# Two decode layers with sliding-window attention: V as the moving operand in seven heads of the first attention, one matmul each for the mask and the q block

## The chip, the cores and the metric

The kernel runs on one core of a Trainium2 chip. The metric is the device time of one execution in microseconds; the time given for a kernel is the median of its runs. The five engines are named as in the profile: PE (TensorE, with PEld for its weight loads), DVE (VectorE), ACT (ScalarE), POOL (GpSimd) and SP (SyncE, which here only issues DMAs).

## What is computed

Four sequences take one decode step through attention, GLU, attention, GLU, with the same weights and the same cache both times:

```python
W = min(4096, max(256, Sk // 4))            # 2048 of 8192 cached positions
q = (x @ wq).reshape(B, Sq, Hq, Dh)         # B 4, Sq 1, Hq 32, Dh 128
k = repeat(k_cache[:, :, Sk - W:, :], 4)    # 8 kv heads, 4 q heads on each
v = repeat(v_cache[:, :, Sk - W:, :], 4)
p = softmax((q @ k.T) * Dh ** -0.5)
attention = (p @ v).reshape(B, Sq, Hq * Dh) @ wo
glu = (sigmoid(g) * u) @ w_down             # g = x @ w_gate, u = x @ w_up, width 1792

x = x + attention(layernorm(x)); x = x + glu(layernorm(x))
x = x + attention(layernorm(x)); x = x + glu(layernorm(x))
```

Everything is bf16 in memory; D is 512. The K window and the V window are 16 MB each, wq and wo 4 MB each, the GLU weights 5.5 MB together.

## The kernel before, in words

**Memory.** One arena of 50 slots of 4 KB per partition (512 KB each) holds what is loaded. Slots 0 to 31 keep the whole K window, loaded once and used by both attentions. The other 18 slots are 9 pairs of 1 MB, given out by a small pool: a load takes a free pair, and the pair goes back when its last reader is done (`done`, `give`, `fill`, lines 450 to 473). The four Wo pairs stay until the second attention has used them. Towards the end of the first attention some loads are given fixed half pairs as homes (`load_half`, line 487): halves of Y (V of head 7, first pair), Z (head 7, second), GA (head 6, first) and GB, a pair that the loads list takes from the pool behind the last Wo load (line 1439). All big loads are issued by SP in the order of one list (lines 1428 to 1453): wq, K two heads ahead of V, Wo every second head, V; then the GLU weights, wq again, the second V pass from head 7 down, the GLU weights again. V of head 7 and parts of head 6 stay on the chip between the two attentions, some of them parked in PSUM by DVE transposes (`stash`, `stash_half`).

**Planning.** Every operation is entered in a plan with an engine, an estimated duration, what it reads and writes, and the PSUM banks that it touches. `_schedule` then makes one fixed order for each engine from estimated times, and `_assign_sync` puts in the waits. On the chip each engine runs its list in order. So an estimate changes the order of instructions, not what they do; SP keeps the list's order whatever the estimates are.

**One head of the first attention** (`attn_first`, line 1171). `k_transpose`: four DVE transposes turn the K of the head (line 854). `q_unit` (834): four matmuls write the q of the head into the four diagonal blocks of a block matrix in PSUM, the zeros with it, and one ACT copy of 128x256 brings it to `qbd`. `softmax_unit` (861): four matmuls of 32 rows add the mask (872), sixteen the scores (883), then DVE takes the maximum in five small steps (896 to 908), and ACT the exponential with the row sums (911). `turn_p` (922): a permutation matmul, an ACT copy and a DVE transpose give the probabilities in the layout that PV needs. `pv_unit` (960): **V is the stationary operand**; 32 matmuls for each of the two V pairs of the head load 128x128 of V as weights and move 8 columns of probabilities (973). Then DVE scales by the reciprocal of the sums (`oe`, 981), four matmuls permute (991), DVE masks (`oq`, 996), and `wo_unit` multiplies by Wo in sixteen matmuls with Wo as weights (1162), collecting in one PSUM bank. The loop prepares the scores of head h+2 before PV of head h.

**One head of the second attention** (`attn_second`, line 1201) for the first seven of its heads is in the wide form. `pv_wide` (1041): **V is the moving operand**; sixteen matmuls take 32 columns of probabilities as weights and move 512 columns of V, four side by side on different columns of the PE array (1055). DVE transposes the 128x512 result (`tv`, 1064), reduces it to its diagonal (`rd`, 1069) and shifts half of it (`sh`, 1071); POOL adds and scales (`ad`, `av`, 1073 and 1076); two matmuls and an ACT copy bring it into the layout for Wo (`tr`, `oc`, 1090 and 1096); `wo_wide` needs four matmuls with Wo moving (1109), collected in another bank that `wo_copy` and `wo_back` fold in at the end (1136, 1146). The last two of the seven use `wo_compact` (1125), sixteen matmuls with Wo as weights. `sums` (1023) does the row sums on POOL with one small f32 matmul, where `sums_old` (936) splits them in three bf16 parts. The wide form's intermediate results live in `wide_buffers`, laid over an arena slot.

## Time and profile before

| | |
|---|---|
| median of the runs | 178.71 us (178.64, 178.71, 178.74) |
| the profiled execution | 178.76 us, of which the span from first to last instruction is 177.0 |
| read from HBM | 70.26 MB |
| DVE in first attention, 20 to 40 and 60 to 80 us | 15.21 and 12.85 of 20 us busy |
| PE in the same stages | 11.35 and 7.60 of 20 us busy |
| DVE in second attention, 130 to 150 us | 18.70 of 20 us busy |
| first attention ends (its last Wo matmuls) | 105.03 us |
| second attention ends (its last Wo matmuls) | 164.73 us |
| last matmul of the kernel | ends about 174.65 us |

How to read it: times in the views are microseconds from the first instruction, so they add up to the span and not to the execution's time. The page cuts the span into 40 slices of 4.43 us and gives each engine's busy share in tenths. A row of a group view gives the line in the kernel, the engine, the operation with its output and inputs, the number of instructions, their busy time, the mean duration of one in ns, the time that the engine stood idle just before them and what it waited for.

### The profile page before, as it was taken

What the parts mean: (1) busy time and instruction counts of PE and PEld (TensorE: products, weight loads), DVE (VectorE), ACT (ScalarE), POOL (GpSimd) and SP (SyncE); (2) the same over time, 40 slices, a digit from 0 to 9 for tenths busy, and PEclk for the clock granted to TensorE, in tenths of its full rate; (3) what the DMA queues carried; (4) which work ended last, traced back from release to release, by engine and by line L of the source; (5) the groups of instructions that cost most, each with busy time, mean ns of one, the idle gap of its engine ahead of it and who ended that gap; (6) DMA issues with size and microseconds to landing.
All of it is one profiled execution on the core that took longest, in us unless ns stands there. A gap on an engine that the chain in (4) does not pass through costs nothing.

```text
span 177.0 us, 3893 instructions
## 1 busy us (share of the span) xinstructions
PE 102.3 (58%) x1641; PEld 55.0 (31%) x1653; DVE 104.6 (59%) x256; ACT 32.7 (18%) x87; POOL 21.6 (12%) x88
## 2 busy tenths in 40 slices
PE   0536236382842634607418866456886999776663
PEld 0203112241431431603404852052323444435322
DVE  7307997838477375594383772304299999742351
ACT  2002031312030210300301101000043365430011
POOL 6100010101010100100100100000011454342000
PEclk9999999999999999999999999999999999975555
DMA  6999999999999999999999999999999999999980
GB/s 179 418 429 428 420 422 416 416 420 426 411 414 429 415 422 418 415 420 426 411 420 428 400 403 403 409 401 387 404 429 409 420 418 422 413 417 405 413 351 28
DMA packets 12882, 70.52 MB, mean 398 GB/s; under 512 B 1336, under 2 KB 1344, under 8 KB 6720
## 3 DMA queue, kind: packets, MB, share of 16 engines
q1 hardware_dynamic: 12856, 70.26, 97.4%
q8 instruction: 13, 0.21, 0.5%
q14 instruction: 5, 0.04, 0.1%
q10 hardware_dynamic: 8, 0.00, 0.0%
HBM read 70.26 MB, written 0.00 MB: 397 GB/s over the span
## 4 chain that ended last, share of the span: by engine, by line
DMA 38%; DVE 32%; PE 18%; issue 4%; SPq 4%; ACT 2%; DVEq 0%; ACTq 0%
DMA arena<-in_B_w_down_dram 15%; DMA arena<-in_A_v_cache_dram 15%; DVE arena L854 11%; PE ps L883 7%; DVE nmax L896 5%; DMA arena<-in_B_w_gate_dram 4%; DMA arena<-in_A_wq_dram 4%; SPq L398 4%; PE ps L973 3%; PE ps L872 2%; DVE nmax L900 2%; DVE mxt L904 2%; DVE ebuf L931 2%; PE ps L1162 2%; DVE arena L1064 2%
## 5 line engine op out<-in xcount | busy, mean ns | idle before, releaser
L854 DVE STREAM_TRANSPOSE arena<-arena 128x1024 f32<-128x1024 f32 x32 | 37.0, 1202 | 0.0
L883 PE MATMUL ps<-arena,qbd 128*32 128x512 bf16 x256 | 25.6, 537 | 0.0
L896 DVE TENSOR_REDUCE nmax<-ps 128x1 f32<-128x512 f32 x16 | 10.8, 675 | 19.4 <-PE ps L883 19.3
L973 PE MATMUL ps<-ebuf,arena 128*128 128x8 bf16 x576 | 17.7, 168 | 7.5 <-DMA arena<-in_A_v_cache_dram 4.4
L872 PE MATMUL ps<-msk_m,msk_s 128*32 128x512 bf16 x64 | 8.6, 526 | 23.1 <-DVE arena L854 21.8
L973 PEld LDWEIGHTS ps<-ebuf,arena 128*128 128x128 bf16 x576 | 16.8, 104 | 9.5 <-DMA arena<-in_A_v_cache_dram 5.5
L911 ACT ACTIVATE prow<-ps,nmax 128x512 bf16<-128x512 f32 x16 | 11.0, 687 | 35.1 <-DVE nmax L908 29.5
L847 ACT CAST qbd<-ps 128x256 bf16<-128x256 f32 x16 | 5.9, 370 | 45.0 <-PE ps L883 35.1
L940 POOL CAST s<-psm 128x1 bf16<-128x1 f32 x9 | 1.7, 187 | 84.0 <-ACT prow L911 84.0
L883 PEld LDWEIGHTS ps<-arena,qbd 128*32 128x32 bf16 x256 | 8.4, 121 | 10.4 <-issue 7.7
L795 PE MATMUL ps<-arena,xn 128*4 128x512 bf16 x64 | 8.5, 572 | 4.9 <-DMA arena<-in_A_wq_dram 4.4
L926 ACT CAST prow<-ps 128x512 bf16<-128x512 f32 x16 | 9.4, 585 | 9.9 <-PE ps L973 2.1
L1342 PE MATMUL ps<-arena,xn 128*4 128x448 bf16 x64 | 7.7, 547 | 4.2 <-DMA arena<-in_B_w_up_dram 1.9
L931 DVE STREAM_TRANSPOSE ebuf<-prow 128x256 f32<-128x256 f32 x16 | 7.0, 435 | 3.8 <-ACT prow L926 3.7
L872 PEld LDWEIGHTS ps<-msk_m,msk_s 128*32 128x32 bf16 x64 | 1.7, 98 | 24.1 <-DVE arena L854 22.7
L773 ACT ACTIVATE lnv<-ps 128x4 f32<-128x4 f32 x4 | 0.7, 173 | 41.0 <-PE ps L769 41.0
L1055 PE MATMUL ps<-arena,ebuf 128*32 128x512 bf16 x112 | 7.9, 405 | 0.2 <-DVE nmax L908 0.2
L842 PE MATMUL ps<-qh,eyew 32*128 32x64 bf16 x64 | 5.6, 217 | 3.7 <-ACT qbd L847 2.4
L807 DVE STREAM_TRANSPOSE ebuf<-ps 128x512 f32<-128x512 f32 x3 | 2.1, 717 | 9.4 <-PE ps L795 9.3
L1351 DVE STREAM_TRANSPOSE ebuf<-ps 128x448 f32<-128x448 f32 x4 | 2.6, 650 | 7.1 <-PE ps L1342 7.1
L1162 PE MATMUL ps<-onp,arena 128*128 128x16 bf16 x144 | 5.3, 175 | 2.5 <-DVE onp L996 2.2
L981 DVE TENSOR_TENSOR onb<-ps,rinv 128x16 bf16<-128x16 f32 x9 | 1.7, 185 | 8.3 <-PE ps L973 8.1
(112 smaller groups left out, 132.2 us busy)
## 6 DMA issues: line engine op xcount, KB each, us to landing
arena<-in_A_v_cache_dram SPq DMA_DIRECT2D x27, 1024.0 KB, 22.4
arena<-in_A_k_cache_dram SPq DMA_DIRECT2D x16, 1024.0 KB, 25.1
arena<-in_A_wq_dram SPq DMA_DIRECT2D x4, 1024.0 KB, 8.0
arena<-in_A_wq_dram SPq DMA_DIRECT2D x8, 512.0 KB, 6.2
arena<-in_A_wo_dram SPq DMA_DIRECT2D x3, 1024.0 KB, 26.2
arena<-in_B_w_down_dram SPq DMA_DIRECT2D x4, 512.0 KB, 6.4
arena<-in_B_w_gate_dram SPq DMA_DIRECT2D x4, 448.0 KB, 8.3
arena<-in_B_w_up_dram SPq DMA_DIRECT2D x4, 448.0 KB, 6.2
```

The costliest lines, as they stand in the source:

```text
L795: last = pe.matmul(ps[32 * hh:32 * hh + NB, qb, :], xn[:, c * NB:(c + 1) * NB], src[:, o + hh * 512:o + (hh + 1) * 512], start=(c == 0), s ...
L854: P.op("vector", "T%d_%d" % (h, t), c_dve(1024), lambda v, v32=v32: v.transpose(v32, v32), r=[("slot", 4 * h + t)], w=[("slot", 4 * h + t)])
L872: last = pe.matmul(ps[32 * gi:32 * gi + 32, bank, :], msk_s[:, :], msk_m[:, :].unsqueeze(1).broadcast_to([128, 256, 2]), start=True, stop= ...
L883: last = pe.matmul(ps[32 * gi:32 * gi + 32, bank, :], qbd[:, q0:q0 + 32], kt[:, cp // 2, cp % 2, jh * NJ:(jh + 1) * NJ, :], start=False, s ...
L896: lambda v: v.tensor_reduce(nmax[:, k2:k2 + 1], ps[:, bank, :], AXX, ALU.max),
L911: lambda a: a.activation(prow[:, :].rearrange("p (m x t) -> p m x t", x=32, t=2), ps[:, bank, :].rearrange("p (m t x) -> p m x t", x=32, t ...
L926: P.op("scalar", "pc" + tag, c_act(512), lambda a: a.copy(prow[:, :], ps[:, pb, :]), r=[("ppb", pb)], w=[("prow",)], banks=(pb,))
L931: P.op("vector", "pt" + tag, c_dve(256), lambda v: v.transpose(et, prow[:, :].bitcast(F32)), r=[("prow",)], w=[("e", k2)])
L973: last = pe.matmul(ps[:, ob, bp * 8:bp * 8 + 8], src[:, j * 128:(j + 1) * 128], ev[:, j % 2, j % 16 // 2, x0:x0 + 8], start=(j == 0), stop ...
L1055: last = pe.matmul(ps[32 * g:32 * g + 32, ob, :], ew[:, g, mq, t], src.rearrange("p (m t d) -> p t m d", t=2, d=128)[:, t], start=(n == 0) ...
L1162: last = pe.matmul(ps[:, WB, c * NR:(c + 1) * NR], tile_ap(s)[:, o + r_ * D + c * 128:o + r_ * D + (c + 1) * 128], ov[:, r_ * NR:(r_ + 1) ...
L1342: last = pe.matmul(ps[32 * g:32 * g + NB, gub[n], 0:NF], xn[:, c * NB:(c + 1) * NB], slot_ap(s)[:, g * NF:(g + 1) * NF], start=(c == 0), s ...
```

## The change

The first attention's heads 0 to 6 use the wide form (`pv_wide`, `sums`, `o_back`, then `wo_wide` for heads 0 to 4 and `wo_compact` for 5 and 6); head 7 keeps the old form. All of them share one wide buffer, a half of pair GB, so GB is taken from the pool before anything is loaded, and its other half is free for a weight half from the start. Homes of the half loads are dealt out anew. The PV of head 5 is issued in two parts, one for each V pair; the other wide heads read both pairs in one operation. All four parts of V of head 7 are parked before its results are scaled.

The mask becomes one matmul with 128 weight columns in place of four with 32. The q of a head becomes one matmul of 64 columns, and four ACT copies put its 32-row blocks on the diagonal of `qbd`, whose zeros are set once at the start and again after the first GLU, which overlays it. Both hold in both attentions; the copies are issued one head ahead in the first. The zeroing of PSUM at the start covers four banks instead of three. Estimates for the first attention are given separately from those for the second (`est`), which bears on the order alone; the wide buffer index is 0 there (`kb`).

```diff
-        msk_s = sb("msk_s", [128, 32], BF16)
+        msk_s = sb("msk_s", [128, 128], BF16)
...
+        def est(tag, first, rest_):
+            return first if tag[0] == "0" else rest_
+
+        def kb(tag, k2):
+            return 0 if tag[0] == "0" else k2
...
-                                  (((Y, 1), (GB, 0), (GB, 1), (GA, 0)), ((GB, 0), (GB, 1), (GA, 0), (Y, 0)))[i][c])
+                                  (((GB, 0), (GB, 1), (GA, 0), (Y, 0)), ((GB, 1), (GA, 0), (Y, 0), (Y, 1)))[i][c])
...
-                                  (((GB, 0), (GB, 1), (GA, 0), (Y, 0)), ((Y, 1), (Z, 0), (GB, 0), (GB, 1)))[nm == "wu"][c])
+                                  (((GB, 1), (GA, 0), (Y, 0), (Y, 1)), ((GB, 0), (Z, 0), (GB, 1), (GA, 0)))[nm == "wu"][c])
...
-        P.op("vector", "zero_o", 1100.0, lambda v: v.memset(ps[:, OBS[0]:WB + 1, :], 0.0), w=[("o0",)], banks=OBS + (WB,))
+        P.op("vector", "zero_o", 1450.0, lambda v: v.memset(ps[:, PBS[1]:WB + 1, :], 0.0), w=[("o0",)], banks=(PBS[1],) + OBS + (WB,))
...
+        P.op("vector", "eye4", 100.0,
+             lambda v: v.tensor_copy(eyew[:, 32:128].rearrange("p (a j) -> p a j", a=3),
+                                     eyew[:, 0:32].unsqueeze(1).broadcast_to([128, 3, 32])),
+             r=[("eyew",)], w=[("eye4",)])
...
-            def e_qx(pe):
-                last = None
-                for a in range(4):
-                    last = pe.matmul(dst[:, :, a * REP:(a + 1) * REP], eyew[32 * hh:32 * hh + 32, 96 - 32 * a:224 - 32 * a],
-                                     src, start=True, stop=True)
-                return last
-            P.op("tensor", "qx" + tag, 250.0, e_qx, r=[("qh", h // 4), ("eyew",)], w=[("cb",)], banks=(CB,))
-            P.op("scalar", "qe" + tag, c_act(256),
-                 lambda a: a.copy(qbd[:, k2 * 256:(k2 + 1) * 256], ps[:, CB, 0:256]),
-                 r=[("cb",)], w=[("q", k2)], banks=(CB,))
+            P.op("tensor", "qx" + tag, 200.0,
+                 lambda pe: pe.matmul(ps[:, CB, 0:64], eyew[32 * hh:32 * hh + 32, :], src, start=True, stop=True),
+                 r=[("qh", h // 4), ("eyew",), ("eye4",)], w=[("cb",)], banks=(CB,))
+            dst = qbd[:, k2 * 256:(k2 + 1) * 256].rearrange("p (x y) -> p x y", y=NR)
+            for a in range(4):
+                P.op("scalar", "qe%d%s" % (a, tag), 200.0,
+                     lambda e, a=a: e.copy(dst[32 * a:32 * a + 32, :, a * REP:(a + 1) * REP],
+                                           ps[32 * a:32 * a + 32, CB, 0:64].rearrange("p (x r) -> p x r", r=REP)),
+                     r=[("cb",)], w=[("q", k2, a)], banks=(CB,))
...
             def e_m(pe):
-                last = None
-                for gi in range(4):
-                    last = pe.matmul(ps[32 * gi:32 * gi + 32, bank, :], msk_s[:, :],
-                                     msk_m[:, :].unsqueeze(1).broadcast_to([128, 256, 2]), start=True, stop=False)
-                return last
+                return pe.matmul(ps[:, bank, :], msk_s[:, :], msk_m[:, :].unsqueeze(1).broadcast_to([128, 256, 2]),
+                                 start=True, stop=False, skip_group_check=True)
...
+            for bps in ((0,), (1,)) if tag == "0.%d" % (NF1 - 2) else ((0, 1),):
+                P.op("tensor", "PV" + tag, est(tag, 1950.0, 16 * tm["pe_row"]), lambda pe, bps=bps: e_pv(pe, bps),
...
+        NF1 = HKV - 1
+
         def attn_first():
+            slot = base[GB]
+            begin = len(P.ops)
+            wide_buffers([slot], P.ops[-1])
+
             def front(h):
                 k_transpose(h)
-                softmax_unit("0.%d" % h, h)
-                turn = lambda: turn_p(0, "0.%d" % h, h % 2, PBS[h % 2])
-                return turn
-
+                softmax_unit("0.%d" % h, h, q=False)
+                if h + 1 < HKV:
+                    q_unit("0.%d" % (h + 1), h + 1, (h + 1) % 2)
+                return lambda: turn_p(0, "0.%d" % h, h % 2, PBS[0], h < NF1)
...
+                pv_wide(tag, h, h % 2, v_tiles[(0, h)])
                 if turn is not None:
                     turn()
-                wo_unit(tag, h, op, h % 2, False, h == HKV - 1)
+                op = late.pop(("tr", tag))()
+                if h < NF1 - 2:
+                    wo_wide(tag, h, op, h % 2, h == 0, h == NF1 - 3)
+                    if h == NF1 - 3:
+                        wo_copy(0)
+                        wo_back(0, False)
+                else:
+                    wo_compact(tag, h, op, h % 2)
+            wide_done()
+            h, tag = NF1, "0.%d" % NF1
+            st = [stash(stashed, (n,)) for n in range(4)]
+            need(Z)
+            op = pv_unit(tag, h, h % 2, v_tiles[(0, h)])
+            oe, oq = named("oe" + tag), named("oq" + tag)
+            oe[0].deps.update(st)
...
+            if not last:
+                P.op("gpsimd", "qbd1", 200.0, lambda g: g.memset(qbd[:, 0:2 * NH], 0.0),
+                     w=[("q", 0, a) for a in range(4)])
...
-        loads.append((GB, lambda s: None))
...
+        base[GB] = pool.alloc()
+        hfree.add(base[GB] + 1)
         fill()
```

## The prediction

> **What bounds the kernel now.** I read the page first: busy shares, the 40 slices, the DMA queues.
>
> ```profile
> span 177.0 us, 3893 instructions
> PE 102.3 (58%) x1641; PEld 55.0 (31%) x1653; DVE 104.6 (59%) x256; ACT 32.7 (18%) x87; POOL 21.6 (12%) x88
> DMA  6999999999999999999999999999999999999980
> GB/s 179 418 429 428 420 422 416 416 420 426 411 414 429 415 422 418 415 420 426 411 420 428 400 403 403 409 401 387 404 429 409 420 418 422 413 417 405 413 351 28
> q1 hardware_dynamic: 12856, 70.26, 97.4%
> q8 instruction: 13, 0.21, 0.5%
> ```
>
> No engine is busy over 59%, while the 16 DMA engines are full in 37 of 40 slices: loads take 97.4% of their span. 70.26 MB at the 415 GB/s of the full slices is 169 us; what is left is the start (first issue at 0.79 us, slice 0 at 179 GB/s) and the tail. So a stage can be shortened without moving the end, unless the queue of loads runs empty, the engines get fewer bytes, or the tail changes. The chain of waits agrees only in part: it names DVE for 32% and PE for 18%, because it follows slot releases through the heads; but the loads so released wait 22 to 27 us in the queue (median issue to landing of the V and K rows), so those links have slack.
>
> Next I looked where the queue is shortest: the timeline at the end of first attention.
>
> ```profile
> 86.42 0.53 SPq L398 DMA_DIRECT2D arena<-in_A_v_cache_dram  x1
> ...
> 94.68 1.87 PE L973 MATMUL ps<-ebuf,arena 128*128 128x8 bf16 x64
> ...
> 95.72 1.30 SPq L398 DMA_DIRECT2D arena<-in_A_wo_dram  x3
> ...
> 97.06 4.95 SPq L398 DMA_DIRECT2D arena<-in_B_w_gate_dram  x4
> ```
>
> The last first-attention V pair is issued at 86.42, just behind head 4's PV; PE waits for that pair until 101.93, so 15 us of transfers are queued. Wo waits for the first half of head 5's PV (the x64, halves of 1 us) and still has 6 us ahead of it. From 100 to 125 us the GLU and q weights land 6 to 8 us after issue at 398 to 405 GB/s: shorter queue, engines still at 101 to 103% in the table by stage.
>
> Last, the tail.
>
> ```profile
> 169.87 0.91 PE L1342 MATMUL ps<-arena,xn 128*4 128x448 bf16 x8 [0.43 <-DMA arena<-in_B_w_up_dram]
> ...
> 172.37 1.02 PE L1383 MATMUL ps<-arena,hT 128*4 128x128 bf16 x32 [1.16 <-DMA arena<-in_B_w_down_dram]
> ...
> 173.62 1.01 PE L1383 MATMUL ps<-arena,hT 128*4 128x128 bf16 x24 [0.22 <-DMA arena<-in_B_w_down_dram]
> ```
>
> PE waits for each of the last loads. Waits of 0.43, then 0.6 (hT ready at 171.75, matmuls at 172.37), then 0.22 give second attention about 1.3 us to be late before the end moves.
>
> **The change, part by part.** Durations are from rows grouped by line and form.
>
> ```profile
> L973 PE MATMUL ps<-ebuf,arena 128*128 128x8 bf16 x576 | 17.7, 168 | 7.5 <-DMA arena<-in_A_v_cache_dram 4.4 <-ACT prow L911 3.1
> L1055 PE MATMUL ps<-arena,ebuf 128*32 128x512 bf16 x112 | 7.9, 405 | 0.2 <-DVE nmax L908 0.2
> L1064 DVE STREAM_TRANSPOSE arena<-ps 128x512 f32<-128x512 f32 x7 | 4.8, 693 | 1.6 <-PE ps L1055 1.5
> L1069 DVE TENSOR_REDUCE arena<-arena 128x32 f32<-128x128 f32 x7 | 2.9, 417 | 0.2
> L1076 POOL TENSOR_TENSOR arena<-arena 64x256 bf16<-64x256 f32 x7 | 4.7, 666 | 0.5
> ```
>
> *PE, first attention.* Per head 64 narrow PV matmuls (2 x 1.02 us) become 16 wide ones (1.05 us in second attention, 1.65 us where the clock is halved). Nearly nothing in time: PE is busy 38 to 61% in these stages, and the end waits for loads.
>
> *DVE.* Per head oe and oq (0.19 + 0.23) go; tv, rd and sh (0.69 + 0.42 + 0.18) come; the reciprocal drops from 0.24 to 0.18. That is +0.8 us on about 7.3 (4 transposes of 1.20, max 0.68, two copies 0.30, 0.25, 0.21, turn 0.44, the 0.42 above and the reciprocal), so 8.1 us per head against 10 us in which its 4 MB land. Hidden; without that cover 7 x 0.8 = 5.6 us.
>
> *POOL and ACT.* POOL per head 0.76 becomes 1.5 (0.31 + 0.30 + 0.25 + 0.67); it idles 84 us on one wait group. Four q copies replace one of 0.37. No row has a 32x64 copy out of PSUM: nearest are 0.18 (L1096, 128x16) and 0.37 (128x256), so four cost 0.7 to 1.5 us; I take 0.8, near the small one. It delays the first S of second attention by about 0.4, inside the 1.3 us. One mask matmul lasts as long as four side by side (0.62 or 0.40), since those overlap: no time. One q matmul for four saves about 0.15 us per head of idle PE. The larger zeroing memset (4 banks for 3, +0.45 us) and eye4 stand before 7 us, under the wq loads that PE awaits until 13.28. The qbd memset lies between the GLU and the next q copies, 10 us on an idle POOL.
>
> *SP's queue.* Same loads and bytes; the pair GB is taken at the start, so 8 pairs turn over instead of 9 and each V load waits for a release one V pair later. The last V pair then waits for head 5's first PV half: near 95.7 instead of 86.42, if PE keeps its order (wide form splits just this head). V pairs land 2.5 us apart (1.05 MB at 418), so the pair before it lands at about 99.4, and 3.7 us remain queued. Cost nothing; each microsecond beyond would cost one. The first weight half GB,1 is free from the start, so one gate load needs no release.
>
> *Instruction fetches.* Matmuls removed: PV 7 x 48 = 336, permutation 28, row sums 21 - 14 = 7, Wo 112 - 52 = 60, masks 48, q 48; added: tr 14, wr 8. Net 505, and 505 weight loads with them: 3294 PE instructions become 2284. q8 moves 0.21 MB in 13 packets for 3294, so 253 each; 2284 need 9. Its 0.5% of 16 engines over 177.0 us is 14.2 engine-us, 1.09 us a packet, on engines that are otherwise full of loads. Four fewer are 4.4 engine-us, spread over 16 engines 0.27 us. This is the only term that touches the bound. Both ends: nothing, if the engine that ends last keeps its fetches; 1.09 us, if it loses one.
>
> The Trainium skill (DMA: Bandwidth & Descriptors, "Why a DMA increments its semaphore by 16 and not by 1") says that the engines of a transfer finish independently and only all 16 mean that the data landed. By that rule the mean of 0.27 never appears as such, and either end does; slices 38 and 39 (351 and 28 GB/s) fit engines that run out at different times.
>
> **Sum.** The profiled execution took 178.76 us: span 177.0 and 1.76 around it; the median is 178.71. 178.76 - 0.27 = 178.5.
>
> **Rivals.** *Faster: the last engine loses a fetch.* 178.76 - 1.09 = 177.7. For it: a fetch occupies one engine for 1.09 us, and the loads wait for all. Against: some five fetches fall into the last 50 us, whose program is nearly unchanged, and one of them suffices to keep the last engine late.
>
> *Slower: the last V pair is released too late.* PE takes instructions in order. Head 4's tail (tr, Wo, a copy of 0.59, four f32 products of 0.95) may stand ahead of head 5's PV, and waits for POOL behind DVE, where the K transposes of head 7 form a block of 4.56 us from 87.80. Then PV ends at 96.8 rather than 95.7 and nothing happens; if its release slips past about 98.2 (99.4 less 1.2 us from an issue to its first data, estimated from the 4 KB output: 0.35 issue and 0.9 wait), the queue runs dry. A slip to 99.0 costs 0.8: 179.5.
>
> *Slower: second attention late.*
>
> ```profile
> 125.36 0.62 PE L872 MATMUL ps<-msk_m,msk_s 128*32 128x512 bf16 x4
> ...
> 132.20 0.40 PE L872 MATMUL ps<-msk_m,msk_s 128*32 128x512 bf16 x4 [0.44 <-DVE arena L593]
> ```
>
> The same four matmuls take 0.62 at 125 and 0.40 at 132 us: PE runs at half rate until about 130, though the page's clock row shows 9 there, and again from 157.7 (0.5). The rows decide. Between, PE was busy 4.00 of 4.00 us (126 to 130); the slower q copies open gaps of some 0.4 us there. If the full rate comes one head later, S (1.73 against 1.11), PV (1.65 against 1.05) and mask cost 1.4 us more for that head, plus 0.4: 1.8 against 1.3 of slack, 179.3; three heads late 182. The Trainium skill (TensorE: Matmul & The Clock Gate, "What's actually happening") has the gate open after a window of about 3.4 us of activity; by that rule the gaps could cost one window, and the trace agrees as far as the busy stretch before 130 goes.
>
> *Nothing happens.* 178.7; within the forecast's band.
>
> **How the numbers follow.** Forecast (0 to 0.35 us less, or unchanged): 0.40. Last engine loses a fetch: 0.34. Late V release: 0.20. Second attention late: 0.06. Differences under 0.2% (0.36 us) can hardly be told from none, so faster 0.34, same 0.40, slower 0.26. The range goes from 177.4 (one fetch and the mean) to 179.8 (a late release by 1.1 us); outside it I leave about 0.16. The forecast's own band is 178.35 to 179.05.
>
> **What would show it.** Right: q8 with 9 packets, PE near 1136 matmuls, q1 still about 70.26 MB, slices at 9 throughout, PE still waiting for B_w_down at the end. Wrong for the V release: an 8 or less near slices 21 to 23 and PE waiting longer for V before 102. Wrong for second attention: L1383 idle on DVE or ACT instead of a load. The forecast fails if loads move at another rate, or if DVE falls behind the K landings.

## The result and the profile after

The changed kernel takes 180.3 us (median; runs from 178.93 to 181.51) against 178.62 us for the kernel before in the same session (178.46 to 179.47): ratio 1.0097, 95% interval 1.0067 to 1.0126. It is slower by 1.7 us, and its runs spread 2.5 times as widely. The profiled execution took 181.01 us: a span of 179.3 and 1.7 around it. Medians are over all runs of a kernel; the ratios leave out its slow runs, those over 1.5% above its fastest (one each of e3, e5 and e12 below).

The page of the changed kernel, the same lines as were shown of before:

```profile
span 179.3 us, 2987 instructions
PE 109.0 (61%) x1148; PEld 44.1 (25%) x1148; DVE 110.1 (61%) x264; ACT 41.6 (23%) x143; POOL 27.1 (15%) x89
DMA  5999999999999999999999999999999999999980
GB/s 187 424 424 435 413 428 419 413 424 413 420 423 416 424 420 419 417 417 422 424 417 430 390 384 369 405 398 345 406 338 369 420 424 424 419 412 405 411 353 19
q1 hardware_dynamic: 12856, 70.26, 97.0%
q8 instruction: 9, 0.15, 0.3%
```

The bytes are the same, the instruction fetches went from 13 to 9 as worked out, and the DMA row still shows 9 in 37 slices. What changed is the row below it: slices 24, 27, 29 and 30 (counted from 0) move 369, 345, 338 and 369 GB/s where the kernel before moved 387 to 429. The same in three stretches; columns are the stretch, its length, busy time of each engine, the granted TensorE clock, the DMA share and, last, GB/s. Kernel before:

```profile
104.00:112.00 8.00, 4.81 (x44) 2.11 (x44) 3.50 (x12) 0.72 (x4) 0.00 (x0) 1.00 1.03 404
121.00:127.00 6.00, 4.47 (x38) 1.64 (x38) 1.71 (x4) 0.75 (x3) 0.00 (x0) 1.00 1.02 386
127.00:138.00 11.00, 8.84 (x116) 3.32 (x110) 9.23 (x26) 3.75 (x9) 1.60 (x6) 1.00 1.03 420
```

Changed kernel:

```profile
104.00:112.00 8.00, 4.91 (x53) 2.16 (x49) 3.83 (x13) 0.72 (x4) 0.00 (x0) 0.50 0.99 372
121.00:127.00 6.00, 3.65 (x20) 1.07 (x20) 2.11 (x4) 1.19 (x6) 0.00 (x0) 0.50 1.01 362
127.00:138.00 11.00, 8.81 (x85) 2.70 (x86) 7.58 (x21) 4.01 (x15) 1.07 (x5) 0.76 1.00 360
```

Against a full rate of 420 GB/s the kernel before leaves (16 x 8 + 34 x 6) KB = 0.33 MB unused in these 25 us, 0.8 us of transfer; the changed one (48 x 8 + 58 x 6 + 60 x 11) KB = 1.39 MB, 3.3 us. The difference, 2.5 us, is as large as the whole loss (1.7 in the medians, 2.25 in the two profiled executions) and a little more. **The DMA share does not show it**: it is 0.99 to 1.01 while a seventh of the rate is gone. Each load is moved in packets, and the packets of these loads usually take 0.16 us (4 KB) or 0.31 us (8 KB). In the changed kernel's trace 15 packets between 121 and 138 us take more than 1.2 us, up to 2.2; in that of before none does. A stalled packet counts as busy.

The clock column does not tell the two kernels apart as it seems to. The trace of before has no clock record ahead of 130.18 us, and the column shows that as 1.00. The matmuls run alike: the sixteen score matmuls of head 7 take 1.93 us in before (from 92.82 us) and 1.90 in the changed kernel (from 93.42 us), where the column shows 0.50. And e2 and e3 below lose time at a mean granted clock of 0.95 and 0.94; before has 0.95, the changed kernel 0.71.

Loads are counted here in SP's order from 0: 38 is the last V pair of the first attention, 39 to 41 wo, 42 to 45 gate, 46 to 49 up, 50 to 53 down, 54 to 61 wq halves, 62 to 64 V halves, from 65 on full V pairs. Each of the 16 DMA engines ends its part of a load with a 4-byte packet, here called its mark. The table counts the marks of all engines together in order of time. It gives the time in us at which all marks due for the loads before have been counted and one more. That is near the end of the load on the first engine, but not the same: the engines are up to 2.6 us apart.

| load | 38 | 43 | 50 | 58 | 61 | 64 | 66 | 79 |
|---|---|---|---|---|---|---|---|---|
| before | 99.53 | 104.69 | 112.81 | 122.56 | 126.74 | 130.48 | 135.49 | 167.06 |
| changed | 99.39 | 104.32 | 113.11 | 122.85 | 127.56 | 131.54 | 138.05 | 169.23 |

Up to load 43 the changed kernel is 0.37 us ahead (0.32 in the mean of the engines); it has had three instruction fetches by then, the kernel before six. Between 43 and 66 it loses 2.9 us by this count, 2.4 to 2.6 in the mean of the engines. What has been lost by then is not made up behind it: the loads of the last 40 us are full pairs with 4 to 18 us of queue, limited by bytes.

These loads have a short **lead**: the time from their issue until the load before is through by this count. In before and in the changed kernel it is 4.8 and 2.0 us for load 44, 4.2 and 2.0 for 45, 2.3 and 1.7 for 48, 2.0 and 1.9 for 59, 2.3 and 1.9 for 65, 2.3 and 1.8 for 66. For all other loads from 36 on it is 2.3 us or more, mostly far more. Two places set it. The first is DVE at the end of the first attention (start, us, what; x3 stands for three in a row). In before the transposes that park V follow each other up to small operations of the old form:

```profile
99.44 1.32 DVE L578 STREAM_TRANSPOSE ps<-arena 128x512 f32<-128x512 f32 x2
100.87 0.19 DVE L981 TENSOR_TENSOR onb<-ps,rinv 128x16 bf16<-128x16 f32 x1
101.10 0.73 DVE L578 STREAM_TRANSPOSE ps<-arena 128x512 f32<-128x512 f32 x1
```

In the changed kernel:

```profile
99.29 0.73 DVE L582 STREAM_TRANSPOSE ps<-arena 128x512 f32<-128x512 f32 x1 [0.89 <-DMA arena<-in_A_v_cache_dram]
99.92 0.67 DVE L1069 STREAM_TRANSPOSE arena<-ps 128x512 f32<-128x512 f32 x1
...
100.99 0.27 DVE L1075 TENSOR_REDUCE arena<-arena 128x32 f32<-128x128 f32 x1
101.30 0.18 DVE L1077 COPY arena<-arena 64x32 f32<-64x32 f32 x1
101.51 1.91 DVE L582 STREAM_TRANSPOSE ps<-arena 128x512 f32<-128x512 f32 x3
```

The transposes of L582 park a V pair in PSUM; the half pairs that they free take gate loads 44 and 45. In the changed kernel the wide tail of head 6 (L1069, L1075, L1077) stands between the first and the second, and both gate loads need a parked half where one did before: the first half of GB is the work space of the wide form now, and every home has moved up by one. So load 44 goes out at 102.33 instead of 99.88. The second place is TensorE and ScalarE at the start of the second attention. The score groups in before:

```profile
126.19 1.93 PE L883 MATMUL ps<-arena,qbd 128*32 128x512 bf16 x16
...
128.90 1.67 PE L883 MATMUL ps<-arena,qbd 128*32 128x512 bf16 x16
```

In the changed kernel:

```profile
127.25 0.60 PE L802 MATMUL ps<-arena,xn 128*4 128x512 bf16 x4 [1.03 <-DMA arena<-in_A_wq_dram]
127.63 1.92 PE L884 MATMUL ps<-arena,qbd 128*32 128x512 bf16 x16
129.48 0.23 PE L845 MATMUL ps<-qh,eyew 32*128 32x64 bf16 x1
...
130.69 1.82 PE L884 MATMUL ps<-arena,qbd 128*32 128x512 bf16 x16 [0.44 <-ACT qbd L850]
```

The scores of units 0 and 1 (L884) free the K slots that loads 65 and 66 take. They end 1.4 and 1.9 us later than before (129.58 and 132.51 against 128.14 and 130.57): a wq piece lands late, and the four copies (L850) are waited for.

### The profile page after: what moved, and what is told of

Read it like the earlier page. It is cut to its first block, busy times and chain, and to the rows that moved or that the text cites. A ratio compares the mean times of both kernels' runs of the same rounds, so it can differ in the third digit from the quotient of the medians.

```text
span 179.3 us, 2987 instructions
## 1 busy us (share of the span) xinstructions
PE 109.0 (61%) x1148; PEld 44.1 (25%) x1148; DVE 110.1 (61%) x264; ACT 41.6 (23%) x143; POOL 27.1 (15%) x89
## 4 chain that ended last, share of the span: by engine, by line
DMA 63%; DVE 24%; PE 8%; issue 2%; SPq 1%; ACT 1%; DVEq 0%
DMA arena<-in_A_v_cache_dram 34%; DMA arena<-in_B_w_down_dram 15%; DMA arena<-in_A_wq_dram 10%; DVE arena L858 5%; DVE nmax L898 3%; DMA arena<-in_B_w_up_dram 3%; PE ps L1058 2%; DVE arena L1069 2%; PE ps L884 2%; DVE ebuf L933 2%; DVE nmax L902 2%; DVE ps L582 1%; DVE mxt L906 1%; DVE arena L597 1%; DVE arena L1075 1%
## 5 line engine op out<-in xcount | busy, mean ns | idle before, releaser
L884 PE MATMUL ps<-arena,qbd 128*32 128x512 bf16 x256 | 25.6, 537 | 0.8 <-ACT qbd L850 0.7
L1058 PE MATMUL ps<-arena,ebuf 128*32 128x512 bf16 x224 | 22.2, 499 | 1.9 <-DMA arena<-in_A_v_cache_dram 1.8
L850 ACT CAST qbd<-ps 32x64 bf16<-32x64 f32 x64 | 12.9, 202 | 19.7 <-PE ps L845 18.6
L874 PE MATMUL ps<-msk_m,msk_s 128*128 128x512 bf16 x16 | 8.4, 524 | 11.5 <-DVE arena L858 11.4
L1097 PE MATMUL ps<-msks,arena 64*128 64x8 bf16 x28 | 2.9, 172 | 17.3 <-POOL arena L1082 16.7
L926 PE MATMUL ps<-prow,perm 128*128 128x512 bf16 x16 | 7.3, 458 | 8.6 <-ACT prow L913 8.3
L1029 POOL TENSOR_SCALAR arena<-sel_r,psm 128x8 f32<-128x8 f32 x14 | 4.3, 309 | 50.8 <-ACT prow L913 49.8
L1069 DVE STREAM_TRANSPOSE arena<-ps 128x512 f32<-128x512 f32 x14 | 9.6, 685 | 1.6 <-PE ps L1058 1.5
L1058 PEld LDWEIGHTS ps<-arena,ebuf 128*32 128x32 bf16 x224 | 7.0, 115 | 13.0 <-issue 10.6
L884 PEld LDWEIGHTS ps<-arena,qbd 128*32 128x32 bf16 x256 | 6.6, 114 | 13.7 <-issue 9.9
L1082 POOL TENSOR_TENSOR arena<-arena 64x256 bf16<-64x256 f32 x14 | 9.3, 667 | 1.1
L1079 POOL TENSOR_TENSOR arena<-arena 64x32 f32<-64x32 f32 x14 | 3.4, 245 | 23.8 <-DVE arena L1077 23.8
```

The source lines that it names most:

```text
L850: lambda e, a=a: e.copy(dst[32 * a:32 * a + 32, :, a * REP:(a + 1) * REP], ps[32 * a:32 * a + 32, CB, 0:64].rearrange("p (x r) -> p x r", ...
L874: return pe.matmul(ps[:, bank, :], msk_s[:, :], msk_m[:, :].unsqueeze(1).broadcast_to([128, 256, 2]), start=True, stop=False, skip_group_c ...
L884: last = pe.matmul(ps[32 * gi:32 * gi + 32, bank, :], qbd[:, q0:q0 + 32], kt[:, cp // 2, cp % 2, jh * NJ:(jh + 1) * NJ, :], start=False, s ...
L1058: last = pe.matmul(ps[32 * g:32 * g + 32, ob, :], ew[:, g, mq, t], src.rearrange("p (m t d) -> p t m d", t=2, d=128)[:, t], start=(n == 0) ...
L1069: P.op("vector", "tv" + tag, est(tag, 720.0, c_dve(512)), lambda v: v.transpose(tv, ps[:, ob, :]), r=[("pso", k2, 0), ("pso", k2, 1)], w=[ ...
L1082: lambda v: v.tensor_tensor(av[0:64, :].rearrange("p (x q e) -> p x q e", x=8, q=4), o32[0:64, :].rearrange("p (q x) -> p x q", x=8).unsqu ...
```

## The experiments

Four accounts were tried first, and the expectations use their letters. **A**: the q copies make the first scores of the second attention late. **B**: the wide form makes the releases at the end of the first attention late. **C**: TensorE comes to its full clock later (in the trace at 132.3 instead of 130.2 us). **Q**: whatever makes them late, the loads between 100 and 133 us have so short a lead that each late release empties the queue. R, F and, from e12 on, B are explained in the expectations that use them; B there is another account than here: the bytes set the time in this stretch too. All ratios are to the kernel before, with 95% intervals.

### e1: the wide form alone

The changed kernel with the q block and the mask of before:

```diff
-                 lambda pe: pe.matmul(ps[:, CB, 0:64], eyew[32 * hh:32 * hh + 32, :], src, start=True, stop=True),
...
+                for a in range(4):
+                    last = pe.matmul(dst[:, :, a * REP:(a + 1) * REP], eyew[32 * hh:32 * hh + 32, 96 - 32 * a:224 - 32 * a],
...
+                 lambda a: a.copy(qbd[:, k2 * 256:(k2 + 1) * 256], ps[:, CB, 0:256]),
...
+                for gi in range(4):
+                    last = pe.matmul(ps[32 * gi:32 * gi + 32, bank, :], msk_s[:, :],
```

> The changed kernel with the old q block (four matmuls, one copy of 128x256) and the old mask (four matmuls); only the wide form of first attention with its buffers, homes and estimates is left of the change. Theory A (the second V pass runs dry: its first full-size loads take the K slots that the first two scores of second attention release, and the four q copies make those scores late): S1 is 0.5 us earlier than with the change, so 178.9 to 179.4. Theory B (the loss arises at the end of first attention, where the wide tail of head 6 stands on DVE among the parking transposes and the third gate load is issued at 102.3 instead of 99.9 us): the whole loss stays, 180.0 to 180.4.

Measured: 180.96 us, 1.0113 (1.0089 to 1.0137). The wide form alone, with its buffers, homes and estimates, brings the whole loss; taking away the copies gains nothing here.

### e2 and e3: the q block alone, the q block and the mask

The kernel before with the new `q_unit` (e2), and with the new mask matmul too (e3):

```diff
+            for a in range(4):                                                                # e2, e3
+                P.op("scalar", "qe%d%s" % (a, tag), 200.0,
+                     lambda e, a=a: e.copy(dst[32 * a:32 * a + 32, :, a * REP:(a + 1) * REP],
+                                           ps[32 * a:32 * a + 32, CB, 0:64].rearrange("p (x r) -> p x r", r=REP)),
...
+                return pe.matmul(ps[:, bank, :], msk_s[:, :], msk_m[:, :].unsqueeze(1).broadcast_to([128, 256, 2]),   # e3
```

> The kernel before with only the q block changed (one matmul, four copies). Theory A: the second score of second attention ends about 0.5 us later than before and the loads behind it too, 179.1 to 179.6. Theory B: no difference from before, 178.4 to 178.8.

> The kernel before with the q block and the mask changed, first attention in its old form. One mask matmul took as long as four side by side in both profiles (0.61 and 0.62 us), so all theories expect what q alone gives: A 179.1 to 179.6, B 178.4 to 178.8.

Measured: e2 180.08 us, 1.0071 (1.005 to 1.0092); e3 181.92 us, 1.0151 (1.0112 to 1.019). So the q block alone is slower too, by more than A gave it, and the mask, which has no time of its own (0.61 us for the one matmul, 0.62 for the four), makes it worse; I did not expect that. In e3's trace up loads 47 and 48 go out at 106.86 and 108.70 us instead of 105.14 and 106.97, with leads of 1.1 and 0.6 us. The trace shows where that delay begins, on TensorE, in the middle of sixteen Wo matmuls:

```profile
103.09 0.30 PE L1160 MATMUL ps<-onp,arena 128*128 128x16 bf16 x5 [0.20 <-DMA arena<-in_A_wo_dram]
105.22 0.44 PE L1160 MATMUL ps<-onp,arena 128*128 128x16 bf16 x11 [1.82 <-issue]
```

TensorE stands for 1.82 us and waits for nothing that the profile shows. The parking transpose behind these matmuls ends 1.7 us later than in before, and load 47 waits for it. e2 has a stop of the same kind, 0.65 us within PV matmuls up to 103.06 us, and its loads 47 and 48 go out 0.7 us later than before. The traces of before and of the changed kernel have no such stop within a group of matmuls there. An instruction fetch goes ahead of each (100.5 us in e2, 102.7 in e3). That TensorE waits for its instructions would fit; no run here separates it. Two parts cost 0.7% and 1.1% alone and 1.0% together: they do not add up, as costs on the path of one resource would.

### e4: three more matmuls for the clock

```diff
-            q_mms(1, 1, WB, (2, 3))
+            q_mms(1, 1, WB, (2,))
+            filler(1)                       # one 128x128 by 128x512 matmul into a free bank
+            q_mms(1, 1, WB, (3,))
+            filler(1)
             q_mms(1, 0, OBS[1], (0,))
+            filler(1)
```

> The changed kernel with three more matmuls of 512 columns into an unused bank (their results are never read), one after each of the third and fourth wq pieces and one after the fifth, so that PE has less idle time ahead of the first scores of second attention. Theory C (PE still at half rate in the first two scores is what makes the releases late: S takes 1.92 and 1.82 us there and 1.11 at the third): the rate doubles before S1 at the latest, S1 ends 0.7 us earlier or more, 179.0 to 179.7, and the runs lie closer together. Theory B: 180.3, as spread as the change.

Measured: 180.83 us, 1.013 (1.0104 to 1.0156). The clock did come earlier: the second score group took 1.11 us instead of 1.82, and load 66 went out at 131.86 us instead of 132.56. The time did not follow, so C falls.

### e5, e6, e7: the late releases made early again

```diff
+            named("wr")[0].deps.update(named("S0.%d" % NF1) + named("PV0.%d" % (NF1 - 2)))   # e5, e7
...
+            named("tv0.%d" % (NF1 - 1))[0].deps.update(st[0:2])                               # e5, e7
...
-            score(0, lambda: q_mms(1, 0, OBS[1], (1,)))                                       # e6, e7
-            qx(1)
+            score(0, lambda: qx(1))
+            q_mms(1, 0, OBS[1], (1,))
```

> The changed kernel with two orders changed at the end of the first attention: the eight float32 matmuls that turn the wide Wo row (L1151, 1.87 us) come behind the scores of head 7 and the second half of head 5's PV product instead of ahead of them, and the second parking transpose (L582) comes ahead of head 6's wide tail. No work is added or left out. Theory Q (the loads between 100 and 133 us have only 2 to 3 us of queue ahead of them, so a late release empties the queue): the first loads of wo pair 3 go out 1.5 to 2.5 us earlier than 97.06 us, the third gate piece 1 us or more earlier than 102.33 us, and load 50 lands 0.3 to 0.7 us earlier; the time falls to 179.5 to 180.0 us. Rival R (the time is lost by something that goes along with the wide form and the q copies, not by these releases): no change, 180.1 to 180.6 us.

> The changed kernel with one order changed at the start of the second attention: the q block of unit 1 is set up ahead of the scores of unit 0, and the second q product of the other half (four matmuls that wait for a wq piece, 127.25 us) comes behind those scores instead of ahead of them. No work is added or left out. Theory Q: the scores of units 0 and 1 end 0.6 to 1.2 us earlier than 129.58 and 132.51 us, the V pairs behind them go out as much earlier, load 66 lands 1.0 to 1.8 us earlier than 138.05 us, and the time falls to 178.8 to 179.6 us. Rival R: no change, 180.1 to 180.6 us.

> The changed kernel with the orders of both of these runs. Theory Q: the gains add up, 178.2 to 179.0 us, at or a little below the kernel before. Rival R: 180.1 to 180.6 us.

Measured: e5 180.3 us, 1.0087 (1.0058 to 1.0116); e6 180.71, 1.0107 (1.0078 to 1.0137); e7 180.76, 1.0132 (1.0079 to 1.0186). None gained what Q said. The releases did move: in e5 load 39 goes out at 94.41 instead of 97.06, but load 44 only at 101.99. The two parking transposes end at 100.69 there, behind the last V pair at 99.3; but load 44 waits for the PV product of head 7 too (L975), whose first half ends at 101.97. So e5 hardly tested account B. In e6 and e7 load 66 has a lead of 4.2 and 4.4 us and lost next to nothing; but the q product that I moved behind the scores releases the slot of load 64, whose lead fell to 1.3 and 1.2, and 65 waits behind it in SP's list. The loss went from one load to its neighbours. Q in the form "earlier releases bring the time back" fails here.

### e8: a pure delay in the kernel before

```diff
-            P.op("scalar", "qe" + tag, c_act(256),
+            for _ in range(3 if tag in ("2.0", "2.1") else 1):
+                P.op("scalar", "qe" + tag, c_act(256),
```

> The kernel before with the copy that sets up the q block done three times instead of once for units 0 and 1 of the second attention (2 x 0.37 us more of ScalarE for each, the same work otherwise). A pure delay: the instructions of every other engine and all loads are as before. Theory Q: the scores of unit 0 end 0.3 to 0.8 us later and those of unit 1 0.6 to 1.5 us later, the V pairs behind them go out as much later and the time rises by about what unit 1 loses, to 179.2 to 179.9 us. The reasoning of the prediction (1.3 us of slack hides it): 178.5 to 178.9 us.

Measured: 179.22 us, 1.0029 (1.0006 to 1.0052). The median rose by 0.6: at the lower edge of Q, and not hidden by 1.3 us of slack. In the profiled execution loads 65 and 66 went out 0.38 and 0.61 us later than before, and yet it took 178.57 us, about what before takes. Four of the ten runs do (up to 178.6), the other six take 179.1 to 180.2: the same delay does not cost the same each time. In e2 loads 65 and 66 go out 0.37 and 0.93 us later, and loads 47 and 48 0.7 us later as well, so the late copies need not be all of its 1.4 us.

### e9, e10, e11: the place of the instruction fetches

Up to here each profile that lost over 2 us in this stretch had a 16 KB fetch of TensorE's instructions (about 1 us on one DMA engine) between 121 and 130 us, and each other had it elsewhere (account F). Tiny matmuls at 15 to 20 us shift the later fetches:

```diff
+        for n_ in range(45 // 5):           # e9, changed kernel: 45; e10, before: 60; e11, before: 20
+            def e_small(pe):
+                for _ in range(5):
+                    last = pe.matmul(ps[:, PBS[0], 0:4], perm[:, :], permo[:, 0:4], start=True, stop=True)
+                return last
```

> The changed kernel with 45 tiny matmuls (128x128 by 128x4, into a bank that nothing reads before it is rewritten) between the q blocks of heads 0 and 1 at 15 to 20 us, where TensorE waits 4.15 us for the key transposes; all else is as it was. They move no load and no order, only the place in the program where TensorE's next 16 KB of instructions are fetched: the fetch that takes one DMA engine for about 1 us at 127.4 us (after 603 recorded matmuls) should come 45 matmuls earlier, near 118 to 120 us, where the loads still have 3 us of queue ahead of them and where the kernel before has its own (118.5 us). Theory F (the fetch in the stretch with the shortest queue makes one of the 16 engines late for every load there, and each use, release and new load waits for it): the loss between 100 and 138 us shrinks from 3.2 us of excess packet time to 1.2 to 1.8, and the time falls to 178.7 to 179.4 us. Theory Q without the fetch (the releases alone, and a latency that differs from load to load): 180.0 to 180.6 us.

> The kernel before with 60 such tiny matmuls at the same place. The fetch at 133.9 us should come at 127 to 129 us, where that of the changed kernel stands, and that of 118.5 us at 113 to 115 us. Theory F: the kernel before becomes slow as the changed one is, 179.8 to 181.0 us. Theory Q without the fetch: 178.5 to 178.9 us.

> The kernel before with 20 such tiny matmuls, as a control: the fetches at 118.5 and 133.9 us should come about 20 matmuls earlier, near 117 and 131 to 132 us, outside the stretch from 121 to 130 us. Theory F: 178.5 to 179.2 us. Theory Q without the fetch: 178.5 to 178.9 us. A rise to 180 us would speak for an effect of the tiny matmuls that neither theory has.

Measured: e9 180.4 us, 1.0102 (1.0066 to 1.0137); e10 178.63, 1.0011 (0.9985 to 1.0036); e11 178.62, 0.9988 (0.9974 to 1.0001). The fetches moved (e9 120.2 us, e10 128.3 us) and the times did not: F falls. The control e11 was to have none in the stretch, but its fetch came at 129.1 us; it stayed as fast as before all the same, which speaks against F once more. In e9 the loads up to 64 land no later than those of before, and the loss comes all the same, 0.8 us at load 65 and 0.4 at load 66.

### e12 and e13: fewer bytes, the same releases

```diff
-                    load_half(half, pair_d(A_v, h, bp)[:, :, n * SLOT:(n + 1) * SLOT], "bw_4k", SLOT, tile)
+                    load_half(half, pair_d(A_v, h, bp)[:, :, n * SLOT:n * SLOT + SLOT // 8], "bw_4k", SLOT // 8, tile)
```

> The changed kernel with the three V halves that follow the wq halves (loads 62 to 64, issued 124.24 to 127.89 us) cut to an eighth of their columns; the products read what the slots held before in the other seven eighths. Every instruction and its order stay; 1.38 MB, some 3.1 us of transfer at 1.27 us a half, are left out. Theory B (the bytes set the time): 177.0 to 177.4 us. Theory Q (the chain release, issue, first data sets when the next full pairs come: load 65 waits for the scores of unit 0 at 129.6 us, load 66 for those of unit 1 at 132.5 us, and the first data come some 2.4 us later): load 66 lands at a mean of 137.0 us where it was 138.4, and the time falls by 0.7 to 1.7 us only, to 178.6 to 179.6 us.

> The kernel before with the same three loads cut to an eighth, the same part left out. Theory B: 175.3 to 175.8 us. Theory Q: load 66 lands at a mean of 135.5 us where it was 136.2, and the time falls by 0.3 to 1.0 us only, to 177.6 to 178.3 us.

Measured: e12 178.54 us, 0.9983 (0.9956 to 1.0009), 1.8 less than the changed kernel; e13 177.51, 0.9944 (0.9914 to 0.9973), 1.1 less than before. Of 3.3 us of transfer left out (1.38 MB at 420 GB/s) only a little over half and a third come back. Both are somewhat over what Q gave and far from B. The rest turns into idle engines, as the same stretch of e13 and e12 shows:

```profile
127.00:138.00 11.00, 8.01 (x116) 3.07 (x110) 9.00 (x26) 3.74 (x9) 1.43 (x6) 1.00 0.83 298
```

```profile
127.00:138.00 11.00, 9.27 (x83) 2.52 (x74) 7.88 (x21) 4.08 (x16) 1.17 (x5) 0.63 0.78 294
```

So once these bytes are out, the chain of release, issue and first data sets the time in this stretch, in both kernels. (The profiled execution of e13 took 179.19 us, the longest of its runs.) The edit itself shortens the lead of load 65, to 0.2 us in e13 and 0.1 in e12. So the two runs show that the chain is 1.1 us shorter than the time in before and 1.8 in the changed kernel, not that it alone sets the time with all bytes there. That is where 1.3 us of slack, read from the tail, did not apply. e13 also gives the latency by itself, since its queue has run empty before the first data of load 65 come. SP's timeline, then stretches of e13:

```profile
128.39 0.54 SPq L398 DMA_DIRECT2D arena<-in_A_v_cache_dram  x1
```

```profile
129.00:129.70 0.70, 0.68 (x12) 0.34 (x16) 0.60 (x4) 0.00 (x0) 0.00 (x0) 1.00 0.01 1
129.70:130.30 0.60, 0.44 (x8) 0.00 (x0) 0.57 (x3) 0.28 (x1) 0.00 (x0) 1.00 0.81 218
130.30:132.00 1.70, 0.82 (x12) 0.36 (x13) 1.70 (x4) 1.22 (x4) 0.00 (x0) 1.00 1.02 347
```

Issued at 128.39, nothing moves until 129.7; the first packets of all 16 engines start at 129.72 to 130.09, 1.33 to 1.70 us behind the issue, and take 0.31 to 0.66 us instead of 0.31. They end 1.8 to 2.0 us behind the issue.

### e14 and e15: an earlier S1

The kernel before (e14) and the changed kernel (e15), each with this edit. S1 stands for the scores of unit 1. e15 has the two edits of e5 as well:

```diff
-            score(0, lambda: q_mms(1, 0, OBS[1], (1,)))
-            qx(1)
+            score(0, lambda: (q_mms(1, 0, OBS[1], (1,)), qx(1)))
```

> The kernel before with the q block of unit 1 set up ahead of the scores of unit 0, the q product of the other half staying ahead of both. Theory Q: S1 ends 0.3 to 0.7 us earlier, load 66 goes out as much earlier, and the time falls by 0 to 0.2 us (the kernel before loses only 0.1 us there): 178.4 to 178.7 us. Theory B: 178.5 to 178.8 us.

> The changed kernel with that order and with the earlier releases of e5_tail_earlier. Theory Q: S1 ends 0.7 to 1.1 us earlier than 132.5 us and load 64 isn't delayed as it was in e6 and e7; of the 3.1 us lost in this stretch 0.6 to 1.2 come back: 179.2 to 179.8 us. Theory B: 180.0 to 180.6 us.

Measured: e14 178.72 us, 1.0011 (0.9996 to 1.0027); e15 180.83, 1.0125 (1.0073 to 1.0177). Nothing to gain in before, as Q had it; in the changed kernel nothing either, against Q, though load 66 goes out at 130.81 us instead of 132.56. No variant that loads all the bytes beats the kernel before.

### What the fifteen profiles say together

Taken over all profiles with the full bytes (15 kernels, loads 44 to 49 and 56 to 67 of each: 270 loads), the time that a load took beyond its bytes (in the mean of its sixteen marks, against the load before), by its lead:

| lead when issued | loads | lost in the mean | share that lost over 0.2 us | most |
|---|---|---|---|---|
| under 2.1 us | 48 | 0.34 us | 60% | 0.94 |
| 2.1 to 2.4 | 38 | 0.14 | 16% | 0.88 |
| 2.4 to 3.2 | 108 | 0.08 | 13% | 1.0 |
| 3.2 and more | 76 | 0.04 | 3% | 0.35 |

And the rate that was missing in the three stretches, in us of transfer as worked out above, tells the time of the same execution: before 0.8 (178.76 us), e11 1.0 (178.49), e8 1.0 (178.57), e2 1.4 (179.75), e10 1.8 (179.32), e14 2.0 (179.65), e9 2.3 (180.26), e15 2.4 (179.69), e4 2.8 (180.81), e5 2.9 (180.14), e7 3.0 (180.94), e3 3.2 (182.5), changed 3.3 (181.01), e6 3.4 (180.95), e1 3.5 (181.16). Subtract the one from the other: 177.3 to 178.4 us for all but e3 (179.3; it also moves 373 GB/s from 112 to 121 us where before moves 405, 0.7 us more). So the place of the loss is shown, and so is its size.

**The stalls sit at the head of a load.** In the 17 profiles 107 packets of loads (behind the first 5 us) take more than 1.2 us. In 80 of them the only packet that can stand just ahead on the same engine is a mark, or there is an idle gap: the packet is the first of its load there. In 13 more a mark is one of two candidates. Of the ordinary packets of the changed kernel from 121 to 138 us, 82 of 1204 are as clear, and 139 more may be. So an engine mostly stalls where it comes to a load before that load's data do. In the changed kernel the stalled first packets of load 65 end 3.7 to 4.7 us behind its issue and those of load 66 3.3 to 3.9 us, where e13 needed 1.8 to 2.0. In before no packet of load 65 stalls; the first starts 2.3 us behind the issue.

**What stays open** is why the first data of such a load come up to 4.7 us behind the issue on some engines, and why a load loses more in the kernels with the wide form at the same lead: load 59, at 1.8 to 2.2 us in nearly all, lost 0.15 to 0.41 us in the kernels with the old first attention and 0.31 to 0.93 in those with the new one. Clock, fetches, the q copies and the order of the releases were each tried and are not enough. That the stalls come by chance there fits the wider spread of the changed kernel's runs, and that e10 with a median of 178.63 has single runs up to 180.83; it is not shown.

## Why the prediction was wrong, step by step

- **What bounds the kernel: right as a whole, wrong in the stage that decided.** The prediction made an exception where "the queue of loads runs empty", looked for the place, found 398 to 405 GB/s and loads landing 6 to 8 us after issue from 100 to 125 us, and then passed over it with "engines still at 101 to 103%", at no price. That is the step that failed: in the three stretches between 104 and 138 us shown above the changed kernel moves too little by 3.3 us of transfer, the kernel before by 0.8. The share of busy time cannot tell a stalled packet from a moving one, and the sign announced for an empty queue ("an 8 or less near slices 21 to 23") could not appear: the DMA row shows 9 where 3.3 us are lost. The GB/s row, the next line of the same fence, could have told it. The time from issue to landing hid how short the queue was: of those 6 to 8 us only 2.0 to 4.8 are lead (loads 44 to 61 of before), and the Wo loads that were given 6 us had 3.8.
- **Second attention late: the slack was read at the wrong end.** The q copies were sized right (0.8 us taken; four of 0.20 in the row, 0.89 with the gaps). "It delays the first S of second attention by about 0.4, inside the 1.3 us": the first two score groups came 1.4 and 1.9 us later, and what they release is loads 65 and 66, 40 us ahead of the tail. The tail's 1.3 us are not at their disposal. e8 adds 0.74 us to those copies alone and pays 0.6 in the median. The rival built on a late second attention has a time near the measured one (179.3), but by the slack of the tail, whose waits did not change (last point).
- **DVE hidden: right per head, not at the seam.** In the heads the extra 0.8 us is covered as said. Behind head 6 the three wide operations stand between two parking transposes, with the gate loads waiting; the half pair that the wide form occupies makes it two loads instead of one. The prediction counted that GB,1 is free from the start and not what GB,0 had been used for. That this seam costs time is argued from the issue times; e5 could not free it.
- **The last V pair: wrong time, right outcome.** It went out at 91.28, not 95.7, and landed as early as before. The rival built on it did not happen; 3.7 us of queue were judged to be enough against a latency of 1.2 us. e13 gives 1.33 us for the start of the first packets on an empty queue, so the estimate was near; what was missing is that loads issued 2 us ahead lose time anyway (table above).
- **Instruction fetches: right.** 9 packets, 1148 recorded matmuls for 1136 worked out, and a gain by load 43 of 0.37 us by the count of marks (0.32 in the mean of the engines), where the sum had 0.27 for the whole run. Three fetches fewer of about 1.06 us on one of 16 engines are 0.2 us of it; where the rest comes from is not shown. The fetches were the only term of the sum, and the gain was lost again 30 us later.
- **Mask and q matmuls at no time: right by their rows, yet e3.** One mask matmul lasts as long as four. That the mask costs time beside the q block (1.0071 to 1.0151) is measured. In e3's profile the delay begins with the 1.82 us for which TensorE stands still (shown above), not with the mask's own time; what makes it stand is not shown.
- **The tail: unchanged.** The last matmuls wait for the same loads as before, only later:

```profile
174.64 1.02 PE L1412 MATMUL ps<-arena,hT 128*4 128x128 bf16 x32 [1.15 <-DMA arena<-in_B_w_down_dram]
175.88 1.01 PE L1412 MATMUL ps<-arena,hT 128*4 128x128 bf16 x24 [0.21 <-DMA arena<-in_B_w_down_dram]
```

The idle times are 1.15 and 0.21 us where they were 1.16 and 0.22. This would have been the check on "where is the slack": a kernel that is late by 2.3 us and waits for the same loads for the same time at its end has lost its time in loads, not in the work behind them.

## What to carry to other kernels

When a kernel is bound by loads, look for the stretch where a load is issued only 2 or 3 us before the DMA engines come to it (here loads with under 2.1 us lost 0.34 us each, those with 3.2 or more 0.04). There an operation that frees a buffer can be on the path, however idle its engine is, and what is lost is not made up later. Moving single releases forward need not bring it back: none of e5, e6, e7 and e15 did. Find the stretch by issue times against landings and by bytes moved, not by the busy share of the DMA engines. An edit that saves work elsewhere but takes a buffer or an order away from that stretch may be paid for there.

## What the runs showed of the hardware

- With an empty queue, the first packets of a 1 MB load start 1.33 to 1.70 us after its issue on SP (e13, e12), all 16 engines within 0.4 us of each other. The Trainium skill (DMA: Bandwidth & Descriptors, "Latency and other measured facts") gives about 0.6 us to the first byte on this path; counted from the end of SP's issuing instruction, which takes 0.54 us, the runs here show 0.79 to 1.16 us.
- Single packets of 0.16 or 0.31 us take 1.2 to 2.2 us, on some engines while the others go on at full pace: 15 in the changed kernel from 121 to 138 us, where leads are short, none from 50 to 121 us or behind 138 us, where most are long. Over all profiles at least 80 of 107 of them are the first packet of a load on their engine. The Trainium skill (DMA: Bandwidth & Descriptors, "Latency and other measured facts") has HBM answering in 0.2 us in the mean and in 2 us at high load; stalls of that size would fit, but no run here separates it.
- A 16 KB instruction fetch takes one DMA engine 0.9 to 1.3 us, every 87 to 167 recorded matmuls in the changed kernel and in before; moving it by 20 to 60 matmuls (e9, e10, e11) did not move the time.
- TensorE stood still for 1.82 us within a group of matmuls in e3 and for 0.65 us in e2 while it waited for nothing that the profile shows.
